# Attention and an ELU feed-forward layer on one core: the order of a batch's first and last pair, halved copies of queries and keys, and a least magnitude that is added inside products

## The chip, the cores and the metric

The kernel runs on one core of a Trainium2 chip. The metric is the device time of one execution in microseconds (us). TensorE (PE, with PEld for its weight loads), VectorE (DVE), ScalarE (ACT), GpSimd (POOL) and SyncE (SP, which issues the transfers) each run their own queue of instructions in order and wait for each other through semaphores.

## The reference

```
scores = q @ k.T / sqrt(64) - log(448)          # q, k, v: 8 batches x 12 heads x 448 x 64, fp32
attn   = 1 / (1 + exp(-scores)) @ v
x      = attn.transpose(0, 2, 1, 3).reshape(3584, 768)
h      = x @ w_in                               # 768 x 2048
g      = where(h > 0, h, exp(min(h, 0)) - 1)
out    = g @ w_out                              # 2048 x 768
```

The sigmoid works on each score by itself, so there is no sum over a row. The two weights come in eight-byte words.

## The kernel before

**Products.** PE multiplies 16-bit numbers. An fp32 operand is split (`split`, L120 to L122) into a high half, written by ACT, and a low half, written by DVE from the source and the high half; a product then takes three matmuls: high by high, low by high, high by low. So that the halves fit, a block is first divided by a power of two near its largest magnitude. `absmax` (L125) finds the maxima per partition (`mx`, and `mt` for queries and keys); `magnitude` (L103) multiplies the unit matrix `eye` by each column of them on DVE (`dg`, L105), and its second part `rest` spreads them over all partitions with one matmul of `ones` by `dg` into `pb` (L110), takes the largest (`al`, L112), puts a floor of 2^-36 under it (L113) and keeps the exponent (`pw`, L114). So a magnitude is DVE, PE, DVE in a row. The weights of the first layer go through `magnitudes` and `sum_magnitude` (L132 to L169), where PE adds up exponents and DVE takes the largest, with the same floor at L165.

**Stages.** A batch has 12 heads in six pairs (hp 0 to 5), a pair four groups of keys (0 to 2 of 128 and a rest of 64). Batch 0 keeps its attention in fp32: PE transposes raw queries and keys into an accumulator `pt` (L337), and one DVE instruction copies both to `early` (L341), from where scores are computed. Beside it the 16 tiles of w_in are loaded and converted; beside batch 0's first layer (`moe1`) w_out is. This prologue is ordered by a scheduler, with its own estimate of times.

From batch 1 on, PE, ACT, DVE and SP run in the order that the code is written in (`manual_schedule`, L690 and after). A batch b is a loop over its six pairs. In each pair: scores of groups 0 and 1 and `soften` for each (sigmoid `sg` on ACT, then the halves `at`, the high one on ACT, L413, the low one on DVE, L414); `third`, which splits queries, keys and values of the next pair (`nat`, `vn`) and turns queries and keys by a transposing transfer; loads of a later pair; some steps of the second layer (`moe2`) of batch b-1; `prepare_pair(n + 2)`, which is `mx`, `mt` and `dg` on DVE; scores and `soften` of groups 2 and 3; more steps; `second`, which is `pb` on PE, `al`, `pw` and the scales; `values` (L433, and L425 for the rest) into `pav`; `finish`, which splits `pav` into `xh`. A step of `moe2` is three matmuls (`po`, L529); `fill` takes a number of them from a stock of 96 in odd batches and 128 in even ones. They are what PE does while ACT and DVE work on a pair. `share` divides what is left by the pairs left. In the last pair `hidden` rescales `xh` (L448 to L451) ahead of the last steps; four steps are kept for after `finish` (`tail`); then `moe1` begins with 16 tiles of 18 matmuls (`ph`, L499), and the batch's own magnitude has its `dg` on DVE ahead of that and its `pb` on PE behind the first tile.

The accumulators: `psc` has two buffers, so scores 3 must wait until ACT has read scores 1.

Of the kernel before, what the change touches and what calls it, by code (L numbers as in the profile page):

```python
# [10 lines left out]
BF16 = mybir.dt.bfloat16  # L11
# [5 lines left out]
ALU = mybir.AluOpType  # L17
# [8 lines left out]
TINY = 2.0**-36  # L26
# [6 lines left out]
def attention_ffn(  # L33
# [9 lines left out]
    nc = tc.nc  # L43
    B, H, S, D = q.shape
    DM, DF = w_in.shape
    P = 128
    NP = H // 2
# [38 lines left out]
    stage, w_in_words = [], []  # L86
    ones = const.tile([P, P], BF16, name="ones")
    nc.vector.memset(ones, 1.0)
    eye = const.tile([P, P], BF16, name="eye")
    nc.vector.tensor_copy(eye, ident)  # L90

# [6 lines left out]
    def magnitude(dst, mx, n):  # L98

        dg = sb.tile([P, n, P], BF16, tag="dg", name="dg", bufs=2)  # L103
        for i in range(n):
            nc.vector.tensor_scalar(dg[:, i], eye, mx[:, i : i + 1], None, op0=ALU.mult)  # L105

        def rest():
            pb = ps.tile([P, 512], F32, tag="pm", name="pb", bufs=3)
            row = pb[:, : n * P].rearrange("p (n x) -> p n x", x=P)
            nc.tensor.matmul(row, ones, dg, start=True, stop=True)  # L110
            al = sb.tile([P, n], F32, tag="al", name="al", bufs=2)
            nc.vector.tensor_reduce(al, row, axis=AX.X, op=ALU.max)  # L112
            nc.vector.tensor_scalar(al, al, TINY, None, op0=ALU.max)  # L113
            nc.vector.tensor_scalar(  # L114
                dst.bitcast(U32), al.bitcast(U32), 0x7F800000, None, op0=ALU.bitwise_and
            )

        return rest
# [13 lines left out]
    def magnitudes(t, lo, hi, hl, sums, start, stop):  # L132


        u, h = t.bitcast(U32), hi.bitcast(F32)


        nc.scalar.activation(t, h, AF.Abs, scale=2.0**-112)


        top = hl.bitcast(U16).rearrange("p a (c t) -> p a c t", t=4)[:, :, :, 1]
        nc.scalar.activation(lo, top, AF.Copy, scale=2.0**-13, bias=2.0**-14 - 0.5)
        nc.vector.scalar_tensor_tensor(
            u, u, 3, lo, op0=ALU.logical_shift_left, op1=ALU.bitwise_or
        )

        top = t.bitcast(BF16).rearrange("p a (c t) -> p a c t", t=2)[:, :, :, 1]
        n = t.shape[1]
        for c in range(n):
            nc.tensor.matmul(  # L150
                sums, ones, top[:, c], start=start and c == 0, stop=stop and c == n - 1
            )
# [8 lines left out]
    def sum_magnitude(dst, sums):  # L161

        m = sb.tile([P, 1], F32, tag="alw", name="alw", bufs=2)
        nc.vector.tensor_reduce(m, sums, axis=AX.X, op=ALU.max)
        nc.vector.tensor_scalar(m, m, TINY, None, op0=ALU.max)  # L165
        nc.vector.tensor_scalar(
            dst.bitcast(U32), m.bitcast(U32), 0x7F800000, None, op0=ALU.bitwise_and
        )
# [125 lines left out]
    def prepare(b, hp, raw, rv, xs):  # L294
# [36 lines left out]
        def transposed(sc):  # L331
            x_scale, s_rest, s_scale = (sc[:, n + i : n + i + 1] for i in range(3))
            if b < EXACT:
                pt = ps.tile([P, 2, 512], F32, tag="psc", name=f"pt{u}", bufs=2)
                pt = pt.rearrange("p a x -> p (a x)")
                for t in range(2 * NC + 1):
                    nc.tensor.transpose(  # L337
                        pt[:, t * P : (t + 1) * P], raw[:, t].rearrange("p h d -> p (h d)"), ident
                    )
                qk = early[:, hp % 2]  # L340
                nc.vector.tensor_copy(qk, pt[:, : 2 * S])  # L341
                return x_scale, 1 / math.sqrt(D), [qk], ([rv], rv[:, 2 * NC :])
            nat = sb.tile([P, 2, 2 * NC + 1, P], F16, tag="nat", name=f"nat{u}")
            for t, n_t, s in (
                (0, NC, sc[:, 1:2]), (NC, 1, s_rest), (NC + 1, NC, sc[:, 2:3])
            ):
                split(
                    nat[:, 0, t : t + n_t], nat[:, 1, t : t + n_t],
                    raw[:, t : t + n_t].rearrange("p t h d -> p t (h d)"), s,
                )  # L350
            qk = sb.tile([P, 2, 2 * NC + 1, P], F16, tag="qk", name=f"qk{u}", bufs=2)
            nc.sync.dma_start_transpose(
                qk.rearrange("p i t x -> p (i t) x"), nat.rearrange("p i t x -> p (i t x)")
            )
            parts = [qk[:, i].rearrange("p t x -> p (t x)") for i in range(2)]

            vn = sb.tile([P, 2, 2 * NC, D], F16, tag="vn", name=f"vn{u}", bufs=2)
            split(vn[:, 0], vn[:, 1], rv[:, : 2 * NC], sc[:, 0:1])
            vr = sb.tile([P, 2, D], F32, tag="vr", name=f"vr{u}", bufs=2)
            nc.gpsimd.tensor_scalar(  # L360
                vr, rv[:, 2 * NC :], sc[:, 0:1], 2.0**ATOP, op0=ALU.mult, op1=ALU.mult
            )
            return x_scale, s_scale, parts, ([vn[:, 0], vn[:, 1]], vr)
# [321 lines left out]
    with tc.manual_schedule(engines={E.PE, E.Activation, E.DVE, E.SP}):  # L685
        for b in range(EXACT, B):
            out_scale(*of_moe2, slice(0, 1 if b == EXACT else NH))
            tiles = moe2(b - 1, g, wo)
            left = NF * NH * (NC + (b - 1) % 2)

            def fill(n):
                nonlocal left
                left -= n
                for _ in range(n):
                    next(tiles, None)

            for hp in range(NP):
                n = b * NP + hp
                share = left // (NP - hp)
                tail = 4 if hp == NP - 1 else 0  # L700
                p = pair_of(n)
                for t in range(2):
                    p.scores(t)
                    p.soften(t)
                third()
                if n + 3 < len(pairs):
                    loaded[n + 3] = load_qk(*pairs[n + 3]), load_v(*pairs[n + 3])

                gap = 8 if hp == 0 else 5
                fill(gap)  # L710
                second = prepare_pair(n + 2)
                for t in range(2, NC + 1):
                    p.scores(t)
                    p.soften(t)
                if b == EXACT and hp < NC:

                    step(3 if hp < NC - 1 else NF)
                if hp == NP - 1:
                    h = hidden(b)
                    next(h)  # L720
                fill(share - gap - tail)
                third = second()
                for t in range(NC + 1):
                    p.values(t)
                p.finish()
                fill(tail)
                if b == EXACT and hp == NC - 1:
                    out_scale(*of_moe2, slice(1, NH))
            of_moe2 = next(h)
# [33 lines left out]
```

## Time and profile before

| | us |
|---|---|
| median of 3 runs | 1271.4 (1270.87 to 1273.9) |
| the profiled execution | 1270.86 |
| its span | 1269.1 |
| PE busy | 1200.2 (95%) |
| DVE busy | 823.4 (65%) |
| ACT busy | 671.8 (53%) |

The span runs from the first to the last instruction of the profile; 1.76 us of the profiled execution lie around it. In a row of the timeline stand the start, the duration, engine, line and operation, the written and read tiles with their shape, how many instructions the row holds, and in brackets the idle time ahead of it and what ended that. Rows of groups have busy time and mean duration in ns, then the idle time ahead. Line numbers in them are those of the kernel before.

### The profile page before, as it was taken

How to read it: one execution, taken by the hardware profiler on the slowest of the kernel's cores; microseconds unless marked ns; L12 is line 12 of the kernel's file. 1: busy time of each engine (PE TensorE's matmuls, PEld its weight loads, DVE VectorE, ACT ScalarE, POOL GpSimd, SP SyncE). 2: the span in 40 equal slices, each digit the busy share in tenths (PEclk: the TensorE clock that was granted, in tenths of full speed). 3: DMA queues.
4: the chain of work that ended last, by engine and by line, in shares of the span. 5: the costliest groups of instructions: out<-in, count | busy, mean ns of one | idle time of the engine just before them, and what ended most of it. 6: DMA issues, size and time to landing. Idle time of an engine off the chain costs nothing.

```text
span 1269.1 us, 19337 instructions
## 1 busy us (share of the span) xinstructions
PE 1200.2 (95%) x7246; PEld 610.5 (48%) x7246; DVE 823.4 (65%) x1872; ACT 671.8 (53%) x1015; POOL 84.1 (7%) x319
## 2 busy tenths in 40 slices
PE   5979868999999999999999999999999999999998
PEld 2324334445555554545455554545455554455565
DVE  5898989765766557775666646885576656765500
ACT  5867777643655337744555436654565435663400
POOL 0011001100000000010000000010000100100000
PEclk9889979999999999999999999999999999999999
DMA  8937423420233103340144201440034401410000
GB/s 229 281 100 222 126 77 80 100 49 1 60 84 89 37 1 83 89 86 1 37 92 92 50 1 43 105 103 7 1 86 92 92 1 22 106 43 7 1 25 26
DMA packets 213407, 89.76 MB, mean 71 GB/s; under 512 B 177472, under 2 KB 209216, under 8 KB 213312
## 3 DMA queue, kind: packets, MB, share of 16 engines
q1 hardware_dynamic: 213312, 88.51, 28.7%
q8 instruction: 57, 0.93, 0.3%
q14 instruction: 38, 0.31, 0.1%
HBM read 58.20 MB, written 11.01 MB: 55 GB/s over the span
## 4 chain that ended last, share of the span: by engine, by line
PE 78%; ACT 8%; DVE 7%; DMA 3%; issue 2%; SPq 2%; DVEq 0%; POOL 0%; ACTq 0%; POOLq 0%
PE ph L499 31%; PE po L529 25%; PE psc L384 7%; PE pav L433 6%; PE po_r L529 5%; PE pav L425 3%; ACT sg L395 2%; DMA stage<-in_moe_w_in_dram 2%; ACT at L413 1%; SPq L262 1%; PE pb L110 1%; ACT L395 1%; ACT e L511 1%; DVE e L514 1%; DMA so<-in_moe_w_out_dram 1%
## 5 line engine op out<-in xcount | busy, mean ns | idle before, releaser
L499 PE MATMUL ph<-xh,wi 128*128 128x448 f16 x2304 | 442.0, 353 | 6.1 <-DVE xh L122 2.4
L529 PE MATMUL po<-wo,g 128*128 128x384 f16 x2304 | 392.9, 328 | 0.0
L529 PEld LDWEIGHTS <-g 128*128 128x128 f16 x2688 | 257.2, 98 | 198.4 <-issue 36.3
L499 PEld LDWEIGHTS <-wi 128*128 128x128 f16 x2304 | 225.3, 98 | 218.4 <-issue 7.6
L511 ACT ACTIVATE e<-ph,msc 128x448 f32<-128x448 f32 x128 | 80.8, 633 | 211.7 <-PE ph L499 211.6
L414 DVE SCALAR_TENSOR_TENSOR at<-sg,at 128x896 f16<-128x896 f32 x126 | 137.2, 1090 | 84.5 <-ACT at L413 84.5
L395 ACT ACTIVATE sg<-psc,bias,sc 128x896 f32<-128x896 f32 (+1 forms) x168 | 166.6, 992 | 1.7
L513 DVE TENSOR_SCALAR e<-e 128x448 f32<-128x448 f32 x128 | 50.3, 394 | 170.8 <-ACT e L511 170.7
L121 ACT ACTIVATE xh<-pav,sc 128x448 f16<-128x448 f32 x48 | 30.3, 632 | 216.7 <-PE pav L425 216.7
L384 PE MATMUL psc<-qk 64*128 64x448 f16 x1008 | 116.6, 355 | 11.4 <-ACT sg L395 11.4
L413 ACT ACTIVATE at<-sg 128x896 f16<-128x896 f32 x126 | 119.8, 951 | 4.1
L121 ACT ACTIVATE g<-e,msc 128x384 f16<-128x384 f32 (+1 forms) x192 | 96.0, 534 | 6.0 <-DVE e L514 4.3
L122 DVE SCALAR_TENSOR_TENSOR g<-e,msc,g 128x384 f16<-128x384 f32 (+1 forms) x192 | 94.6, 521 | 0.6
L514 DVE SCALAR_TENSOR_TENSOR e<-ph,msc,e 128x448 f32<-128x448 f32 x128 | 87.3, 683 | 4.0
L384 PEld LDWEIGHTS <-qk 64*128 64x128 f16 x1008 | 41.7, 97 | 89.7 <-issue 60.2
L433 PE MATMUL pav<-at,vn 128*64 128x448 f16 x756 | 80.2, 357 | 0.0
L324 POOL TENSOR_SCALAR sc<-pw 128x1 f32<-128x1 f32 x42 | 12.4, 295 | 843.5 <-DVE pw L114 790.9
L529 PE MATMUL po_r<-wo,g 128*128 128x384 f16 x384 | 64.7, 326 | 0.0
L122 DVE SCALAR_TENSOR_TENSOR xh<-pav,sc,xh 128x448 f16<-128x448 f32 x48 | 32.7, 680 | 48.7 <-ACT xh L121 48.7
L433 PEld LDWEIGHTS <-vn 128*64 128x64 f16 x756 | 39.4, 110 | 50.0 <-issue 27.8
L122 DVE SCALAR_TENSOR_TENSOR nat<-raw,sc,nat 128x384 f16<-128x384 f32 (+1 forms) x126 | 59.1, 524 | 0.0
L121 ACT ACTIVATE nat<-raw,sc 128x384 f16<-128x384 f32 (+1 forms) x126 | 58.8, 529 | 0.0
(103 smaller groups left out, 852.7 us busy)
## 6 DMA issues: line engine op xcount, KB each, us to landing
stage<-in_moe_w_in_dram SPq DMA_DIRECT2D x16, 768.0 KB, 6.6
raw<-in_q_dram SPq DMA_DIRECT2D x96, 96.0 KB, 3.1
raw<-in_k_dram SPq DMA_DIRECT2D x96, 96.0 KB, 2.6
rv<-in_v_dram SPq DMA_DIRECT2D x48, 192.0 KB, 2.7
out_dram<-o SPq DMA_DIRECT2D x48, 192.0 KB, 2.1
wo<-in_moe_w_out_dram SPq DMA_DIRECT2D x19, 384.0 KB, 4.1
so<-in_moe_w_out_dram SPq DMA_DIRECT2D x13, 384.0 KB, 4.3
raw<-in_q_dram SPq DMA_DIRECT2D x48, 32.0 KB, 2.4
```

Source lines behind the costliest of these rows:

```text
L121: nc.scalar.mul(hi, src, s)
L122: nc.vector.scalar_tensor_tensor(lo, src, s, hi, op0=ALU.mult, op1=ALU.subtract)
L384: nc.tensor.matmul(psc[:, j, :S] if g < NC else psc[rows[j], 0, :S], kk[rows[j], o], qq[rows[j], :S], start=(n == 0), stop=(n == len(parts ...
L395: a = nc.scalar.activation(sg[:, :nb], psc[:, :nb, :S], AF.Sigmoid, bias=bias, scale=self.s_scale)
L413: nc.scalar.mul(hi, sg, 2.0**ATOP)
L414: nc.vector.scalar_tensor_tensor(lo, sg, 2.0**ATOP, hi, op0=ALU.mult, op1=ALU.subtract)
L433: nc.tensor.matmul(pav[rows[j], :S], vv[i][:, j * NC + g], sg[k][:, j], start=(g == 0 and n == 0), stop=False,)
L499: nc.tensor.matmul(ph[:, :S], wi[:, wj, c, f * P : (f + 1) * P], xh[:, c, xj], start=(n == 0), stop=(n == 3 * NK - 1),)
L511: a = nc.scalar.activation(e, ph[:, :S], AF.Exp, scale=inv)
L513: nc.vector.tensor_scalar(e, e, 1.0, -1.0, op0=ALU.min, op1=ALU.add)
L514: nc.vector.scalar_tensor_tensor(e, ph[:, :S], inv, e, op0=ALU.mult, op1=ALU.max)
L529: nc.tensor.matmul(po[:, :HM], lh(gj, f), wo[:, i, f, wj], start=(n == 0), stop=(n == 3 * NF - 1),)
```

## The change

Three things change.

The floor under a magnitude goes into the arithmetic: `dg` becomes `eye` times the maximum plus 2^-36 in the same instruction, and for w_in one more matmul of `ones` by a tile of 2^-36 opens the accumulation. The floor instructions go, except for w_out, whose sums are 384 wide.

The copy of batch 0's queries and keys is made in two halves, queries on ACT and keys on DVE.

The order in the main loop: the first pair takes 11 steps and not 8 at its first fill, and three more in all; there `prepare_pair` comes behind scores and `soften` of groups 2 and 3, and `second` moves into the second pair, between scores 0 and 1 and their `soften`. The last pair has no tail: all its steps come ahead of `pb`. The steps by pair become 19, 15, 15, 15, 16, 16 in odd batches (16 each before) and 24, 20, 21, 21, 21, 21 in even ones (21, 21, 21, 21, 22, 22 before).

```diff
@@ -86,6 +86,8 @@
     stage, w_in_words = [], []
     ones = const.tile([P, P], BF16, name="ones")
     nc.vector.memset(ones, 1.0)
+    tiny = const.tile([P, P], BF16, name="tiny")
+    nc.gpsimd.memset(tiny, TINY)
     eye = const.tile([P, P], BF16, name="eye")
     nc.vector.tensor_copy(eye, ident)
 
@@ -102,7 +104,10 @@
 
         dg = sb.tile([P, n, P], BF16, tag="dg", name="dg", bufs=2)
         for i in range(n):
-            nc.vector.tensor_scalar(dg[:, i], eye, mx[:, i : i + 1], None, op0=ALU.mult)
+
+            nc.vector.tensor_scalar(
+                dg[:, i], eye, mx[:, i : i + 1], TINY, op0=ALU.mult, op1=ALU.add
+            )
 
         def rest():
             pb = ps.tile([P, 512], F32, tag="pm", name="pb", bufs=3)
@@ -110,7 +115,6 @@
             nc.tensor.matmul(row, ones, dg, start=True, stop=True)
             al = sb.tile([P, n], F32, tag="al", name="al", bufs=2)
             nc.vector.tensor_reduce(al, row, axis=AX.X, op=ALU.max)
-            nc.vector.tensor_scalar(al, al, TINY, None, op0=ALU.max)
             nc.vector.tensor_scalar(
                 dst.bitcast(U32), al.bitcast(U32), 0x7F800000, None, op0=ALU.bitwise_and
             )
@@ -146,6 +150,10 @@
 
         top = t.bitcast(BF16).rearrange("p a (c t) -> p a c t", t=2)[:, :, :, 1]
         n = t.shape[1]
+        if n > 1:
+
+            nc.tensor.matmul(sums, ones, tiny, start=True, stop=False)
+            start = False
         for c in range(n):
             nc.tensor.matmul(
                 sums, ones, top[:, c], start=start and c == 0, stop=stop and c == n - 1
@@ -162,7 +170,8 @@
 
         m = sb.tile([P, 1], F32, tag="alw", name="alw", bufs=2)
         nc.vector.tensor_reduce(m, sums, axis=AX.X, op=ALU.max)
-        nc.vector.tensor_scalar(m, m, TINY, None, op0=ALU.max)
+        if sums.shape[1] > P:
+            nc.vector.tensor_scalar(m, m, TINY, None, op0=ALU.max)
         nc.vector.tensor_scalar(
             dst.bitcast(U32), m.bitcast(U32), 0x7F800000, None, op0=ALU.bitwise_and
         )
@@ -338,7 +347,8 @@
                         pt[:, t * P : (t + 1) * P], raw[:, t].rearrange("p h d -> p (h d)"), ident
                     )
                 qk = early[:, hp % 2]
-                nc.vector.tensor_copy(qk, pt[:, : 2 * S])
+                nc.scalar.copy(qk[:, :S], pt[:, :S])
+                nc.vector.tensor_copy(qk[:, S:], pt[:, S : 2 * S])
                 return x_scale, 1 / math.sqrt(D), [qk], ([rv], rv[:, 2 * NC :])
             nat = sb.tile([P, 2, 2 * NC + 1, P], F16, tag="nat", name=f"nat{u}")
             for t, n_t, s in (
@@ -696,34 +706,40 @@
 
             for hp in range(NP):
                 n = b * NP + hp
-                share = left // (NP - hp)
-                tail = 4 if hp == NP - 1 else 0
+                share = left // (NP - hp) + (3 if hp == 0 else 0)
                 p = pair_of(n)
                 for t in range(2):
                     p.scores(t)
+                if hp == 1:
+                    third = second()
+                for t in range(2):
                     p.soften(t)
                 third()
                 if n + 3 < len(pairs):
                     loaded[n + 3] = load_qk(*pairs[n + 3]), load_v(*pairs[n + 3])
 
-                gap = 8 if hp == 0 else 5
+                gap = 11 if hp == 0 else 5
                 fill(gap)
-                second = prepare_pair(n + 2)
+
+                if hp:
+                    second = prepare_pair(n + 2)
                 for t in range(2, NC + 1):
                     p.scores(t)
                     p.soften(t)
+                if not hp:
+                    second = prepare_pair(n + 2)
                 if b == EXACT and hp < NC:
 
                     step(3 if hp < NC - 1 else NF)
                 if hp == NP - 1:
                     h = hidden(b)
                     next(h)
-                fill(share - gap - tail)
-                third = second()
+                fill(share - gap)
+                if hp:
+                    third = second()
                 for t in range(NC + 1):
                     p.values(t)
                 p.finish()
-                fill(tail)
                 if b == EXACT and hp == NC - 1:
                     out_scale(*of_moe2, slice(1, NH))
             of_moe2 = next(h)
```

On DVE, at the start of batch 3 (hp 0; a tile's name ends in its batch and pair, and `at2` is group 2's), before:

```order
L122 SCALAR_TENSOR_TENSOR vn3_1_4696<-rv1_85,sc3_1_4205,vn3_1_4696 128x384
L125 TENSOR_REDUCE mx3_2_4736<-rv0_83 128x1
L125 TENSOR_REDUCE mt3_2_4738<-raw3_2_4090 128x7
L307 TENSOR_REDUCE mx3_2_4736<-mt3_2_4738 128x2
L310 TENSOR_TENSOR mx3_2_4736<-mx3_2_4736,mt3_2_4738 64x1 x2
L105 TENSOR_SCALAR dg_4744<-eye_81,mx3_2_4736 128x128 x3
L414 SCALAR_TENSOR_TENSOR at23_0_4757<-sg23_0_4755,at23_0_4757 128x896
L537 TENSOR_SCALAR o2_0_0_4793<-po2_0_0_4711,osc2_4659 128x384
L112 TENSOR_REDUCE al_4798<-pb_4796 128x3
L113 TENSOR_SCALAR al_4798<-al_4798 128x3
L114 TENSOR_SCALAR pw3_2_4743<-al_4798 128x3
```

and now:

```order
L126 SCALAR_TENSOR_TENSOR vn3_1_4681<-rv1_87,sc3_1_4207,vn3_1_4681 128x384
L424 SCALAR_TENSOR_TENSOR at23_0_4739<-sg23_0_4737,at23_0_4739 128x896
L129 TENSOR_REDUCE mx3_2_4751<-rv0_85 128x1
L129 TENSOR_REDUCE mt3_2_4753<-raw3_2_4080 128x7
L316 TENSOR_REDUCE mx3_2_4751<-mt3_2_4753 128x2
L319 TENSOR_TENSOR mx3_2_4751<-mx3_2_4751,mt3_2_4753 64x1 x2
L108 TENSOR_SCALAR dg_4759<-eye_83,mx3_2_4751 128x128 x3
L547 TENSOR_SCALAR o2_0_0_4778<-po2_0_0_4696,osc2_4644 128x384
L126 SCALAR_TENSOR_TENSOR xh3_3918<-pav3_0_4791,sc3_0_4010,xh3_3918 128x448
L129 TENSOR_REDUCE xs3_3919<-xh3_3918 128x1
L117 TENSOR_REDUCE al_4830<-pb_4828 128x3
```

The low half of group 2 (`at23_0`) moves ahead of the next-but-one pair's maxima and `dg`; `al`, which waits for that pair's `pb`, moves behind `xh` of the first pair.

On PE, where that `pb` (`pb_4796` before, `pb_4828` now) stands, before:

```order
L529 MATMUL po2_0_0_4711<-wo_966,g_917 128x384
L110 LDWEIGHTS ones_79
L110 MATMUL pb_4796<-dg_4744,ones_79 128x384
L433 LDWEIGHTS vn3_0_4085
L433 MATMUL pav3_0_4811<-at03_0_4672,vn3_0_4085 64x448
```

and now:

```order
L394 MATMUL psc13_1_4821<-qk3_1_4679 128x448
L115 LDWEIGHTS ones_79
L115 MATMUL pb_4828<-dg_4759,ones_79 128x384
L539 LDWEIGHTS g_917
L539 MATMUL po2_1_0_4781<-wo_965,g_917 128x384
```

It stood between the first pair's last step and its values; it stands now behind the second pair's scores 0 and 1, ahead of that pair's first step.

On DVE at the end of batch 3 (hp 5; `rr` and `xs` belong to the rescaling), before:

```order
L450 TENSOR_SCALAR xh3_3924<-xh3_3924,rr3_5617 128x896 x5
L451 TENSOR_TENSOR xs3_3925<-xs3_3925,rr3_5617 128x5
L112 TENSOR_REDUCE al_5648<-pb_5646 128x3
L113 TENSOR_SCALAR al_5648<-al_5648 128x3
L114 TENSOR_SCALAR pw4_1_5591<-al_5648 128x3
L318 RECIPROCAL sc4_1_5652<-pw4_1_5591 128x3
L282 TENSOR_TENSOR xs4_5412<-xs4_5412,pw4_1_5591 128x1
L285 RECIPROCAL xs4_5412<-xs4_5412 128x1
L122 SCALAR_TENSOR_TENSOR xh3_3924<-pav3_5_5661,sc3_5_5315,xh3_3924 128x448
L125 TENSOR_REDUCE xs3_3925<-xh3_3924 128x1
L537 TENSOR_SCALAR o2_2_1_5696<-po2_2_1_5568,osc2_4659 128x384
```

and now:

```order
L460 TENSOR_SCALAR xh3_3918<-xh3_3918,rr3_5597 128x896 x5
L461 TENSOR_TENSOR xs3_3919<-xs3_3919,rr3_5597 128x5
L547 TENSOR_SCALAR o2_2_1_5638<-po2_2_1_5548,osc2_4644 128x384
L117 TENSOR_REDUCE al_5643<-pb_5641 128x3
L118 TENSOR_SCALAR pw4_1_5571<-al_5643 128x3
L327 RECIPROCAL sc4_1_5646<-pw4_1_5571 128x3
L291 TENSOR_TENSOR xs4_5393<-xs4_5393,pw4_1_5571 128x1
L294 RECIPROCAL xs4_5393<-xs4_5393 128x1
L126 SCALAR_TENSOR_TENSOR xh3_3918<-pav3_5_5655,sc3_5_5296,xh3_3918 128x448
L129 TENSOR_REDUCE xs3_3919<-xh3_3918 128x1
L466 TENSOR_REDUCE rr3_5597<-xs3_3919 128x1
```

The eviction of the last steps (`o2_2_1`), which stood behind `xh`, now stands ahead of `al`, and the floor (L113) is gone.

On ACT in the prologue, rows now, with what each waits for (`pt_1` is the second pair's accumulator, `stage` and `wi` belong to w_in):

```order
L142 ACTIVATE stage<-stage 128x768 [waits DMAHW3_49]
L146 ACTIVATE stage<-stage 128x768
L125 ACTIVATE wi<-stage,swi_155 128x6x128 [waits Pool_49]
L142 ACTIVATE stage<-stage 128x768 [waits DMAHW4_49]
L146 ACTIVATE stage<-stage 128x768
L350 COPY early<-pt_1_192 128x448 [waits PE_49]
L405 ACTIVATE sg_0_209<-psc_0_206,bias 128x896 [waits PE_49]
```

and on DVE, around the other half of the same copy:

```order
L291 TENSOR_TENSOR xs_114<-xs_114,pw_1_180 128x1 [waits DVE_49]
L147 SCALAR_TENSOR_TENSOR stage<-stage 128x768 [waits DMAHW4_49,Activation_49]
L294 RECIPROCAL xs_114<-xs_114 128x1 [waits DVE_49]
L351 COPY early<-pt_1_192 128x448 [waits Activation_49]
L172 TENSOR_REDUCE alw<-si_226 128x1 [waits PE_49]
L165 SCALAR_TENSOR_TENSOR stage<-stage 128x768
```

The copy of the queries is in ACT's queue behind the work on a further tile of w_in, and the copy of the keys on DVE waits for ACT.

## The prediction

> **What bounds the kernel now.** I read the page's totals first, then busy time by stretch of the span.
>
> ```profile
> span 1269.1 us, 19337 instructions
> PE 1200.2 (95%) x7246; PEld 610.5 (48%) x7246; DVE 823.4 (65%) x1872; ACT 671.8 (53%) x1015; POOL 84.1 (7%) x319
> 0.00:98.00 98.00, 72.86 (x358) 29.74 (x359) 77.66 (x203) 63.75 (x81) 8.10 (x33) 0.93 0.71 198
> 98.00:200.00 102.00, 80.98 (x424) 38.87 (x423) 90.12 (x196) 80.73 (x147) 11.42 (x29) 0.91 0.46 137
> 200.00:1202.00 1002.00, 983.64 (x6083) 504.39 (x6081) 648.09 (x1461) 525.10 (x783) 64.56 (x259) 1.00 0.25 55
> ```
>
> A stretch's columns are its length, then busy time of PE, PEld, DVE, ACT and POOL, the granted clock, DMA share and GB/s. Two regimes are to be seen. Up to 200 us no engine is full, and VectorE (DVE) is the busiest: 77.66 of 98 in the prologue (batch 0's attention and w_in's conversion) and 90.12 of 102 in batch 0's first FFN stage. From 200 on, in the main loop, TensorE (PE) works 983.64 of 1002 us: only its idle 18.4 us can be won there. So I listed PE's waits in that stretch in order of time. These rows stand for them, with the first and the last of each kind; column two is the duration, the bracket the idle time ahead and what ended it.
>
> ```profile
> 260.77 0.32 PE L110 MATMUL pb<-dg,ones 128*128 128x384 bf16 x1 [1.90 <-DVE dg L105]
> 850.92 0.32 PE L110 MATMUL pb<-dg,ones 128*128 128x384 bf16 x1 [1.90 <-DVE dg L105]
> 327.49 0.76 PE L384 MATMUL psc<-qk 64*64 64x448 f16 x6 [1.22 <-ACT sg L395]
> 917.64 0.76 PE L384 MATMUL psc<-qk 64*64 64x448 f16 x6 [1.22 <-ACT sg L395]
> 480.01 0.76 PE L384 MATMUL psc<-qk 64*64 64x448 f16 x6 [1.03 <-ACT sg L395]
> 1070.17 0.76 PE L384 MATMUL psc<-qk 64*64 64x448 f16 x6 [1.03 <-ACT sg L395]
> 486.75 0.32 PE L110 MATMUL pb<-dg,ones 128*128 128x384 bf16 x1 [1.97 <-DVE dg L105]
> 781.02 0.32 PE L110 MATMUL pb<-dg,ones 128*128 128x384 bf16 x1 [1.97 <-DVE dg L105]
> 1076.90 0.32 PE L110 MATMUL pb<-dg,ones 128*128 128x384 bf16 x1 [1.97 <-DVE dg L105]
> ```
>
> They lie only in the pairs that the change reorders. The last pair (hp 5) of batches 1, 3 and 5 waits 1.9 for dg; the first pair (hp 0) of 2, 4 and 6 waits 1.22 for scores 3; the first pair of 3, 5 and 7 waits 1.03 for scores 3 and 1.97 for dg. That is 3×1.9 + 3×1.22 + 3×(1.03+1.97) = 18.4.
>
> **The first pair.** Its three added steps of moe2 must fill these waits. What a step lasts, and what DVE and ACT do at batch 3's first pair:
>
> ```profile
> 480.70 4.07 PE L529 MATMUL po<-wo,g 128*128 128x384 f16 x24
> 483.77 0.95 ACT L413 ACTIVATE at<-sg 128x896 f16<-128x896 f32 x1
> 483.84 0.68 DVE L125 TENSOR_REDUCE mx<-rv 128x1 f32<-128x512 f32 x1
> 486.11 0.58 DVE L105 TENSOR_SCALAR dg<-eye,mx 128x128 bf16<-128x128 bf16 x3
> 486.61 1.08 DVE L414 SCALAR_TENSOR_TENSOR at<-sg,at 128x896 f16<-128x896 f32 x1
> 488.13 0.55 DVE L112 TENSOR_REDUCE al<-pb 128x3 f32<-128x384 f32 x1
> 487.00 1.89 PE L433 MATMUL pav<-at,vn 128*64 128x448 f16 x18
> 489.77 1.31 PE L384 MATMUL psc<-qk 64*128 64x448 f16 x12
> ```
>
> 24 matmuls are 8 steps, 4.07/8 = 0.51 each. Three more ahead of scores 2 and 3 are 1.53 us, above both 1.03 and 1.22: those waits go, and the last step of the pair ends 0.5 later, at 485.27 for 484.77 (480.70+4.07). No pb follows now but the values. They need at2's low half only for their last third, at 485.27 + 2/3×1.89 = 486.5. ACT has the high half at 484.72 (483.77+0.95), and the low half, now ahead of mx, takes 1.08: done at 485.8, 0.7 early. The 1.97 goes.
>
> What is late next is dg: from mx's start to dg's end DVE takes 486.69−483.84 = 2.85, so 485.8+2.85 = 488.65. PE asks for it after values (1.89), the remainder's matmuls and two scores (1.31): 485.27+1.89+0.95+1.31 = 489.4. It is hidden by 0.7; were it later, the excess would count in each of six batches. On DVE, al (0.55) and five small operations behind it wait for that pb and now stand ahead of the second pair's own splits. That can make those start up to half a us late, 3 us in six batches; I take nothing, since ACT's splits of the same pair, one after another, reach DVE's queue later still.
>
> **The last pair.** All 11 steps stand ahead of pb, not 7: 4×0.51 = 2.04 covers 1.9. The price is the lost tail between values and the first FFN stage, seen at batch 2's end:
>
> ```profile
> 416.41 2.11 PE L529 MATMUL po_r<-wo,g 128*128 128x384 f16 x12
> 417.49 0.67 DVE L122 SCALAR_TENSOR_TENSOR xh<-pav,sc,xh 128x448 f16<-128x448 f32 x1
> 419.31 0.26 DVE L105 TENSOR_SCALAR dg<-eye,rr 128x128 bf16<-128x128 bf16 x1
> 418.36 3.57 PE L499 MATMUL ph<-xh,wi 128*128 128x448 f16 x18
> 421.77 0.22 PE L110 MATMUL pb<-dg,ones 128*128 128x128 bf16 x1
> ```
>
> The four steps (2.11) stood behind the values, which end at 416.41; now the FFN's first tile does. It uses the last pair's xh only in the last of its six parts, 5/6×3.57 = 3.0 after its start. xh's low half came at 418.16, 1.75 after the values: free. Magnitude's dg came at 419.57, 3.2 after them, and pb is asked for 3.4 after the tile's start (421.77−418.36): free too, by 0.2. If it slips, 0.3 in each of seven batches is 2 us.
>
> **Shares.** 96 steps are now 19, 15, 15, 15, 16, 16 in odd batches, where each pair had 16; even ones have 24, 20, 21, 21, 21, 21. Does a pair of 15 hide the chain scores, ACT, DVE, dg? At batch 3's third pair:
>
> ```profile
> 513.43 0.58 DVE L105 TENSOR_SCALAR dg<-eye,mx 128x128 bf16<-128x128 bf16 x3
> 514.07 0.32 PE L110 MATMUL pb<-dg,ones 128*128 128x384 bf16 x1
> ```
>
> dg ends at 514.01 and pb starts at 514.07: with 16 steps PE comes just as dg does. With 15 it must wait for the step it lacks: about 0.5 for hp 2 and for hp 3. The second pair has an extra pb (0.32) from the first, so it loses 0.17. That is −1.13 in batches 3, 5, 7 and −1.0 in batch 1. Pairs of 20 and more have 2 us in hand.
>
> Sum of the loop: batch 1, 1.9−1.0 = 0.9; 2, 4 and 6, 3×1.22 = 3.7; 3 and 5, 1.03+1.97+1.9−1.13 = 3.8 each; 7, 3.0−1.13 = 1.9. Together −14.1.
>
> **One half-clock window.** Behind the 1.97 wait at 781, and not behind the other two, the same matmuls were slow:
>
> ```profile
> 781.35 2.54 PE pav L433 x18
> 783.88 1.79 PE pav L425 x2
> 488.82 1.02 PE L425 MATMUL pav<-sg,vr 128*128 128x448 f32 x2
> ```
>
> 2.54 against 1.89 and 1.79 against about 0.9 net: 1.5 lost. Without the wait I expect none: −1.5, between 0 and that. The Trainium skill, "TensorE: Matmul & The Clock Gate", section "Why this matters for your kernels", asks for an idle gap of about 3 us before the clock drops. By it the window would have another cause and stay, and the sum would be 1.5 higher; this trace shows a drop in one of three waits of 1.97, so I side with the row.
>
> **The start of batch 1** has two waits of its own, while w_out's last halves are converted:
>
> ```profile
> 196.46 0.74 PE L384 MATMUL psc<-qk 64*128 64x448 f16 x6 [2.51 <-ACT sg L395]
> 198.43 1.17 PE L384 MATMUL psc<-qk 64*64 64x448 f16 x6 [1.23 <-ACT sg L395]
> ```
>
> The three more steps could cover 1.5 of the 3.74; against it, the conversions' halves stand behind the reordered dg. I take −0.5, from −3.7 to +2.
>
> **Prologue.** The diff turns six copies on DVE into halves on two engines and drops the small floor ops.
>
> ```profile
> L341 DVE COPY early<-pt 128x896 f32<-128x896 f32 x6 | 6.5, 1090 | 8.2 <-PE pt L337 8.0
> L113 DVE TENSOR_SCALAR al<-al 128x3 f32<-128x3 f32 (+1 forms) x56 | 9.2, 164 | 1.6
> L121 ACT ACTIVATE xh<-pav,sc 128x448 f16<-128x448 f32 x48 | 30.3, 632 | 216.7 <-PE pav L425 216.7
> L122 DVE SCALAR_TENSOR_TENSOR xh<-pav,sc,xh 128x448 f16<-128x448 f32 x48 | 32.7, 680 | 48.7 <-ACT xh L121 48.7
> 21.42 0.90 ACT L142 ACTIVATE stage<-stage 128x768 uint32<-128x768 uint16 x1
> 17.77 1.09 DVE L341 COPY early<-pt 128x896 f32<-128x896 f32 x1 [0.96 <-PE pt L337]
> ```
>
> A half on either engine costs about 0.6 (632 and 680 ns for such a PSUM read). DVE saves 6×(1.09−0.6) = 2.9 and, with 22 floors (16 tiles, 6 pairs) at 0.16, 3.5: at most −6.4, if every bit counts. But the changed order has each DVE half wait for the ACT half, so the pair takes 1.2 in a row where 1.09 stood, and ACT's second copy stands behind the third w_in tile, whose part ends at 22.32 where the copy began at 17.77: +4.55 if it were on the path. DVE is full through most of the prologue, so freed time should count somewhat: −1, between −6.4 and +4.6. The Trainium skill, "ScalarE: Activation LUTs", section "Rules for kernel authors", would leave plain arithmetic on VectorE, up to about three times faster per element there in bf16. By that an ACT half would be an estimated 1.6 us, and the six copies 6.6 longer in total; the two rows above, 632 on ACT and 680 on DVE, do not agree for fp32 from PSUM. From 98 to 200 and in dg's added operand I take nothing.
>
> Sum: −14.1−1.5−0.5−1.0 = −17.1. The profiled execution took 1270.86 (span 1269.1 and 1.76 around), so 1253.8; the median of the runs is 0.5 above it, so 1254.
>
> **Rivals.**
> Prologue delays. Each copy that comes k times late on ACT's queue costs 4.55 on the path of batch 0. Two give back 9 us: 1264, chance 0.14 for one or two (from 1259). Three or four end at 1268 to 1273, no change: 0.05. The chip is slower only from five on: six give 27.3−1 above 1254, about 1281, since scores of batch 0, and w_in's conversion behind them, start that late: 0.04. For it: ACT runs its instructions in order. Against: in the trace ACT worked 63.75 of 98 us, so most copies find it free.
> More gain. If a 15-step pair loses nothing (PE's latency there being shorter than I read) 4.4 comes back, and with −6.4 for the prologue it is 1244: 0.11 for 1249 or less.
> dg slower. The added operand could put dg in a slower form: +0.1 on each of three in some 18 pairs without slack, 5.4, so 1259. Nothing in the trace shows it; 0.05 within the main case.
> The change does not do what it says in one place: the two halves do not run side by side. This is priced above.
>
> **How the numbers follow.** Main case 1250 to 1259 with 0.66, at 1254. Range 1245 to 1265: it holds the main case, one or two late copies and most of the further gain; about 0.17 is outside. A measurement here tells 0.3%, 3.8 us, from no change: faster is below 1267.6 (0.66+0.14+0.11 = 0.91), same up to 1275.2 (0.05), slower 0.04.
>
> **What would show it.** Right: no waits above 0.5 us ahead of pb or scores 3 in first and last pairs; new waits of 0.5 ahead of pb in hp 2 and hp 3 of odd batches; no half-clock window at batch 5's start; the first main-loop pair within 5 us of its old place. Wrong: a prologue ending over 5 us later, waits for dg at hp 1 or in the FFN's first tile, or dg over 0.3 us each.

## The result: the loop gained what was forecast, and the prologue gave a third of it back

The kernel with the change takes 1260.77 us (1259.97 to 1260.92), the one before 1272.62 beside it: a ratio of 0.9906, with a 95% interval of 0.9889 to 0.9924. So it is faster, by 11.85 us; 1254 was forecast. The profiled execution took 1260.89 with a span of 1259.1; against the span of before, 1269.1, that is 10.0 less, where 17.1 was forecast. (The profiled execution of before, 1270.86, lies 1.76 under the median beside it, so the traces show some 1.9 less gain than the medians.)

The page's totals after the change, and its busy time by stretch (length; PE, PEld, DVE, ACT, POOL; clock, DMA share, GB/s):

```profile
span 1259.1 us, 19310 instructions
PE 1199.5 (95%) x7262; PEld 609.6 (48%) x7262; DVE 813.9 (65%) x1800; ACT 675.1 (54%) x1021; POOL 97.0 (8%) x320
0.00:98.00 98.00, 68.14 (x343) 27.46 (x344) 70.33 (x165) 66.89 (x87) 9.13 (x32) 0.95 0.73 197
98.00:200.00 102.00, 85.81 (x451) 41.62 (x449) 87.72 (x196) 74.89 (x139) 10.11 (x24) 0.93 0.44 135
```

In the first 98 us DVE is busy 70.33 for 77.66 before: the work was taken off it (and some now falls behind 98), but no time came of that. To see where time went, take one instruction that every batch has once, and call its start the batch's mark: the `pb` of the batch's own magnitude, behind the FFN's first tile. Batch 0's mark is called the prologue's end below. Of PE's timeline before the change, batches 0 to 5:

```profile
102.14 0.22 PE L110 MATMUL pb<-dg,ones 128*128 128x128 bf16 x1
269.05 0.22 PE L110 MATMUL pb<-dg,ones 128*128 128x128 bf16 x1
421.77 0.22 PE L110 MATMUL pb<-dg,ones 128*128 128x128 bf16 x1
563.33 0.22 PE L110 MATMUL pb<-dg,ones 128*128 128x128 bf16 x1
716.05 0.22 PE L110 MATMUL pb<-dg,ones 128*128 128x128 bf16 x1
859.21 0.22 PE L110 MATMUL pb<-dg,ones 128*128 128x128 bf16 x1
```

And with the change:

```profile
107.78 0.22 PE L115 MATMUL pb<-dg,ones 128*128 128x128 bf16 x1
273.26 0.22 PE L115 MATMUL pb<-dg,ones 128*128 128x128 bf16 x1
424.68 0.22 PE L115 MATMUL pb<-dg,ones 128*128 128x128 bf16 x1
562.69 0.22 PE L115 MATMUL pb<-dg,ones 128*128 128x128 bf16 x1
714.12 0.22 PE L115 MATMUL pb<-dg,ones 128*128 128x128 bf16 x1
852.13 0.22 PE L115 MATMUL pb<-dg,ones 128*128 128x128 bf16 x1
```

The differences tell the story. The prologue ends 5.64 later (107.78 for 102.14). From there to batch 1's mark takes 165.48 for 166.91, 1.4 less. Batch 2 takes 151.42 for 152.72 (−1.30), batch 3 138.01 for 141.56 (−3.55), batch 4 151.43 for 152.72 (−1.29), batch 5 138.01 for 143.16 (−5.15). Batches 6 and 7 give 1.28 and 1.63 in the same way. Together −10.0.

In the loop, PE's waits of before are gone, and new ones stand where the prediction put them: ahead of `pb` in hp 1, 2 and 3 of batch 3.

```profile
501.70 0.32 PE L115 MATMUL pb<-dg,ones 128*128 128x384 bf16 x1 [0.58 <-DVE dg L108]
515.35 0.32 PE L115 MATMUL pb<-dg,ones 128*128 128x384 bf16 x1 [0.43 <-DVE dg L108]
529.00 0.32 PE L115 MATMUL pb<-dg,ones 128*128 128x384 bf16 x1 [0.43 <-DVE dg L108]
```

### The profile page after: what moved, and what is told of

Its sections match the earlier page's. It is cut to its first block, busy times and chain, and to the rows that moved or that the text cites. A ratio compares the mean times of both kernels' runs of the same rounds, so it can differ in the third digit from the quotient of the medians.

```text
span 1259.1 us, 19310 instructions
## 1 busy us (share of the span) xinstructions
PE 1199.5 (95%) x7262; PEld 609.6 (48%) x7262; DVE 813.9 (65%) x1800; ACT 675.1 (54%) x1021; POOL 97.0 (8%) x320
## 4 chain that ended last, share of the span: by engine, by line
PE 73%; DVE 10%; ACT 7%; DMA 5%; issue 3%; SPq 2%; POOL 1%; DVEq 0%; ACTq 0%; POOLq 0%
PE ph L509 31%; PE po L539 20%; PE psc L394 6%; PE pav L443 6%; PE po_r L539 5%; PE pav L435 3%; ACT sg L405 3%; DMA stage<-in_moe_w_in_dram 1%; ACT at L423 1%; DVE mt L129 1%; DVE mx L129 1%; DVE nat L126 1%; DMA wo<-in_moe_w_out_dram 1%; PE pb L115 1%; DVE dg L108 1%
```

## The experiments

**Parts alone.** Theory: the reordered loop gained as forecast, and the two edits that reach into the prologue lost 6 us there, above all the halves. Rival: the floor edits lose it. A third, that the reordered loop itself delays w_out's conversion, was put to the first run. For each run, the part of the diff that it keeps (the order of pairs; the halves; the floors):

```diff
+                share = left // (NP - hp) + (3 if hp == 0 else 0)
...
+                gap = 11 if hp == 0 else 5
```

> Only the order of the first and last pair is changed; floors and the single copy stay as before. Theory (the main loop gained what was forecast, and 6 us were lost ahead of it by the two edits in the prologue): 16 to 17 us faster than before, about 1255, with the prologue row for row as before (batch 0's own pb near 102.1). Rival (the reordered loop itself starts 6 us late, since batch 1's first pair delays w_out's conversion): about 10 us faster, as the whole change.

Measured: 1258.41, ratio 0.9881 (0.9868 to 0.9895): 14.9 less than the 1273.33 of before in that series, a little short of the 16 to 17 expected. The prologue ended at 102.73, and up to 98 us every engine's queue has the order of before. So the loop didn't lose the 6 us, and the order of pairs alone is at least as good as the whole change.

```diff
-                nc.vector.tensor_copy(qk, pt[:, : 2 * S])
+                nc.scalar.copy(qk[:, :S], pt[:, :S])
+                nc.vector.tensor_copy(qk[:, S:], pt[:, S : 2 * S])
```

> Only the copy of batch 0's queries and keys is halved between ACT and DVE. Theory (the halves make the scheduler lay the prologue's queues anew, with a w_out load ahead of the third pair's loads, and the copies wait for ACT): 5 to 7 us slower than before, batch 0's own pb near 107 to 109. Rival (the floor edits do it): within 1 us of before.

Measured: 1277.93, ratio 1.0045 (1.0031 to 1.0058), 4.6 slower; prologue's end at 110.12. The rival falls. The theory has the direction; both its numbers are just missed, 4.6 for 5 to 7 and 110.12 for 107 to 109.

```diff
+                dg[:, i], eye, mx[:, i : i + 1], TINY, op0=ALU.mult, op1=ALU.add
...
-            nc.vector.tensor_scalar(al, al, TINY, None, op0=ALU.max)
...
+            nc.tensor.matmul(sums, ones, tiny, start=True, stop=False)
```

> Only the floor is moved into dg and into the sums of w_in. Theory: between 0 and 3.5 us faster than before (22 operations of 0.16 us leave DVE in the prologue). Rival (the floor edits move the prologue's queues for the worse): 5 to 7 us slower.

Measured: 1275.89, ratio 1.002 (1.001 to 1.003), 2.6 slower; prologue's end at 106.75. The theory missed, and the rival's 5 to 7 was too much: this edit too delays the prologue, though on DVE it only takes operations off (PE gets 16 short matmuls more). By the sum of the three parts the whole would be 14.9−4.6−2.6 = 7.7 faster; it is 11.85. About half of the 4.2 between them lies in the loop: with the new order of pairs, batches 3, 5 and 7 take 138.01, 138.01 and 137.43 from mark to mark without the floor and 138.77, 138.78 and 137.97 with it, 2.1 less together, while with the old order batch 3 takes 141.54 without it and 141.56 with it. The rest may come of something that each part sets anew: the scheduler's order.

```diff
+                nc.scalar.copy(qk[:, :512], pt[:, :512])
+                nc.vector.tensor_copy(qk[:, 512:], pt[:, 512 : 2 * S])
```

> The whole change, but the copy is cut at column 512, where the accumulator's first bank ends, so that ACT and DVE read different banks. If the loss in the prologue is that the two halves run one after the other (about 0.6 us in each of six pairs, and what hangs on it): 3 us or more faster than the whole change, about 1257. If it is where ACT's half and the loads stand in their queues: within 2 us of it, 1259 to 1262.

Measured: 1254.23 (1253.85 to 1254.98), ratio 0.9852 (0.9839 to 0.9865), 6.5 faster than the whole change and the fastest of all. It looked like the price of two reads one after the other. But this cut, too, had given the scheduler a new order, so the run didn't tell the two apart. Nor do the reads overlap in it: in all six pairs DVE's half starts after ACT's has ended.

**The order written out.** For that, the next kernels keep their instructions and take the queue order from another kernel. Ahead of the main loop each instruction of the five engines gets a dependency of order alone on the one that stands ahead of it in that other kernel (1,276 to 1,370 of them; those that the other kernel doesn't have are placed by the scheduler):

```diff
+        for a, b in zip(queue, queue[1:]):
+            tc.add_manual_dep(seen[b], a, mybir.DependencyInfo(
+                mybir.DependencyClass.NoSync, mybir.DependencyReason.DATA), ...)
```

The theory is now that the order of the queues sets the prologue; its rivals, that an edit costs by itself.

> Floors moved into dg and into w_in's sums as in the floor-only run (2.6 us slower), but all that is ordered by the scheduler stands in every engine's queue in the order of the kernel before. Theory (the scheduler's new order costs, not the edit): 0 to 3.5 us faster than before. Rival (the added operand or the extra matmul costs by itself): 2 to 3 us slower, as unpinned.

Measured: 1275.04, ratio 1.0014 (1.0001 to 1.0026).

> Queries copied by ACT and keys by DVE as in the halves-only run (4.6 us slower), with every other instruction in the order of before; DVE's half stands where the whole copy stood, and the scheduler places ACT's half alone. Theory (new order): within 1.5 us of before. Rival (two reads one after the other, and ACT's queue, cost by themselves): 4 to 6 us slower, as unpinned.

Measured: 1274.16, ratio 1.0015 (1.0003 to 1.0027).

> As the pinned halves, but cut at column 512 so that the two engines read different banks of the accumulator. If the reads one after the other cost: 2 to 4 us faster than the pinned halves. If only the order of the queues counts: within 1 us of them.

Measured: 1275.31, ratio 1.0018 (1.0005 to 1.003).

These three were less clear than hoped. In the order of before, the halves cost 1.2 by the medians and not 4.6, for the theory. The pinned floors are 2.1 slower by the medians, against the 0 to 3.5 faster that the theory expected. The cut at 512 is 1.2 slower than the pinned halves, but says nothing on parallel reads, for it has none: DVE's half still waits for ACT's and starts as that ends (19.91+0.56 = 20.47).

```profile
19.91 0.56 ACT L394 COPY early<-pt 128x512 f32<-128x512 f32 x1
20.50 0.56 DVE L395 COPY early<-pt 128x384 f32<-128x384 f32 x1 [3.59 <-ACT early L394]
```

Why it waits wasn't tried. So no run here has the two reads side by side, and what that would gain stays open. Kernels with the old loop also spread widely (before from 1270.65 to 1277.19 in this series), those with the new one by 1 to 4 us. The spread goes with the clock: of the 55 executions of before beside these experiments, the 6 with a mean granted clock of 0.981 took 1276.5 in the median, the 18 at 0.983 took 1273.86 and the 12 at 0.985 took 1272.07. Differences of 1 to 2 us between kernels with the old loop are therefore not settled by these medians; so I went on with the new loop.

> The whole change with the cut at column 512, and the instructions ahead of the main loop in the order of before. Theory: the loop's gain of about 15 us and, with nothing lost ahead of it, 1255 to 1258. Rival (the scheduler's own order with that cut, 19 us faster than before, was luck that the order of before doesn't have): as well 1255 to 1258; under 1254 would say that floors and parallel halves gain by themselves.

Measured: 1259.59 (1258.72 to 1260.42), ratio 0.9897 (0.9882 to 0.9911). Above the 1255 to 1258 that was expected, and 5.4 above the same instructions in the scheduler's order for them. That pair is the cleanest answer so far: the instructions are the same, and only their order ahead of the loop differs.

> The whole change with its own cut at 448, and all that stands ahead of the main loop in the queue order that the scheduler had made for the cut at 512 (1254.2). Theory (the order of the queues sets the prologue): 1254 to 1256. Rival (two reads of one bank, one after the other, cost by themselves): 1258 to 1261.

Measured: 1255.38 (1254.42 to 1255.42), ratio 0.9859 (0.9844 to 0.9874). The whole change, unaltered, is 5.4 faster when its prologue stands in another order, and the ranges of the two don't meet. The rival's 1258 to 1261 doesn't come: with its reads one after the other, the change still reaches 1255.38. What such reads cost isn't priced by the 1254.23 of the cut at 512, for there they are one after the other too.

> The whole change with its own cut at 448, and the prologue in the queue order of before. Theory: 1258.5 to 1260, as the cut at 512 in that order (1259.6) and the order alone (1258.4). Rival (one read after the other costs by itself): 1261 or more.

Measured: 1259.42 (1257.21 to 1260.31), ratio 0.9889 (0.9875 to 0.9904). As the theory had it, and the rival's 1261 or more falls.

> Only the reordered pairs, with the old floors and the single copy on DVE, in that same queue order of the prologue. Theory (order alone): 1254 to 1256, against 1258.4 in the order of before. Rival (the work taken from DVE is what gained): 1258 to 1260.

Measured: 1261.56 (1259.77 to 1263.04), ratio 0.9909 (0.9894 to 0.9924). The theory in its plain form falls here, and the time is above the rival's 1258 to 1260 too: the good order doesn't help the old instructions, it costs them 3 us against the 1258.41 in their own. By the traces they lose it in the prologue, which ends at 106.49 for 102.73. Against the change in that order they lose another 2.2 in batches 3, 5 and 7, where they still have the floor. An order is good for the instructions that it was made for. Why these lose in it wasn't tried.

By instructions and order, all with the new loop:

| | order of before | order made for the cut at 512 | the scheduler's own |
|---|---|---|---|
| old floors, one copy | 1258.41 | 1261.56 | as the first column |
| the change, cut at 448 | 1259.42 | 1255.38 | 1260.77 |
| the change, cut at 512 | 1259.59 | 1254.23 | as the second column |

The table has the loop in it, where the floor alone is worth 2.1. By the traces, ahead of batch 1's mark, the change at 448 comes to 272.25 in the first order and 267.78 in the second, the old instructions to 268.83 and 271.00. So it is neither the order nor the instructions but the pair of them: either order is 3 us worse for the other's instructions. Of the 4.5 between the two orders of the change, 1.4 lies ahead of batch 0's mark (104.81 for 103.38) and 3.0 behind it, in the stretch where w_out is converted.

**Where the order bites.** The whole change in its own order loses most of its 5.4 ahead of batch 0's mark, and here one can look for the place. Up to 73.5 us it and the same change in the other order are level (scores at 73.63 and 73.43). Then, in its own order, by engine (SP's rows have the issue and what held it; `raw` and `rv` are loads of queries, keys and values, `stage` of w_in):

```profile
61.96 8.15 SPq L190 DMA_DIRECT2D stage<-in_moe_w_in_dram  x2
70.21 0.50 SPq L256 DMA_DIRECT2D rv<-in_v_dram  x1
79.42 0.62 SPq L275 DMA_DIRECT2D raw<-in_k_dram  x1
76.14 0.98 ACT L405 ACTIVATE sg<-psc,bias 128x896 f32<-128x896 f32 x1
86.54 0.63 ACT L405 ACTIVATE sg<-psc,bias 128x448 f32<-128x448 f32 x1 [4.46 <-PE psc L394]
80.30 0.69 DVE L129 TENSOR_REDUCE mx<-rv 128x1 f32<-128x512 f32 x1 [3.01 <-DMA raw<-in_k_dram]
81.83 0.25 DVE L108 TENSOR_SCALAR dg<-eye,mx 128x128 bf16<-128x128 bf16 x1
82.13 0.26 PE L115 MATMUL pb<-dg,ones 128*128 128x128 bf16 x1 [1.39 <-DVE mx L319]
```

The same instructions in the order made for the cut at 512 (line numbers are about 50 higher, for the table of the order):

```profile
60.23 0.53 SPq L239 DMA_DIRECT2D stage<-in_moe_w_in_dram  x1
67.33 0.37 SPq L305 DMA_DIRECT2D rv<-in_v_dram  x1
69.59 0.37 SPq L239 DMA_DIRECT2D stage<-in_moe_w_in_dram  x1
75.23 0.62 SPq L324 DMA_DIRECT2D raw<-in_k_dram  x1
73.72 0.99 ACT L454 ACTIVATE sg<-psc,bias 128x896 f32<-128x896 f32 x1
75.68 0.69 DVE L179 TENSOR_REDUCE mx<-rv 128x1 f32<-128x512 f32 x1
77.61 0.25 DVE L158 TENSOR_SCALAR dg<-eye,mx 128x128 bf16<-128x128 bf16 x1
79.57 0.23 PE L165 MATMUL pb<-dg,ones 128*128 128x128 bf16 x1
103.38 0.22 PE L165 MATMUL pb<-dg,ones 128*128 128x128 bf16 x1
```

In the slower order (the whole change's own) two loads of w_in stand ahead of the values' load on SP and hold its queue for 8.15 us (probably until a staging buffer is free, which the rows don't show); the values' load is issued at 70.21 for 67.33 and the last keys at 79.42 for 75.23. On DVE, which works in order, the maxima wait 3.01 for a load (80.30 for 75.68; the profile names the keys' load, though `mx` reads `rv`), so `dg` is late, PE's `pb` waits 1.39, and the scores that stand behind `pb` on PE come so late that ACT idles 4.46. On ACT the sigmoid comes 2.4 later, behind conversions of w_in. The prologue ends at 107.78 for 103.38. None of it is the price of an instruction.

Two things weaken this reading. PE's granted clock was half from 75.34 to 85.58 in the slower order and from 74.12 to 77.53 in the other, so the same four matmuls of `pav` take 1.76 at 83.81 there and 0.97 at 80.90 here; how much of the 4.4 is the clock, and how much of the clock comes of the waits, isn't separated. And a prologue's end is that of one execution: the next run has the good order and the instructions of the cut at 512, and its profiled execution, the longest of five at 1259.47, ends its prologue at 106.99 where the kernel that the order comes from ended at 103.21. What shows the order's price is the times of the runs; the rows show where it can arise.

**One step moved.** The fastest kernel with one step less in the first pair and one more in hp 1 of odd batches:

```diff
-                share = left // (NP - hp) + (3 if hp == 0 else 0)
+                share = left // (NP - hp) + (2 if hp == 0 else 1 if hp == 1 and b % 2 else 0)
...
-                gap = 11 if hp == 0 else 5
+                gap = 10 if hp == 0 else 5
```

> The kernel with the cut at 512 in its own queue order, with one step less in a batch's first pair (10 at its first fill) and one more in the second pair of odd batches, so that odd batches have 18, 16, 15, 15, 16, 16. By the waits in the whole change's trace (0.58 ahead of pb in the second pair, 0.43 in each of the next two): the 0.58 goes in each of three or four odd batches, 1.5 to 2.3 us faster than 1254.2. Rival (the first pair has no step to give, scores 3 or dg wait again): no gain, or up to 2 us slower.

Measured: 1256.81 (1255.75 to 1259.47), 2.6 slower than 1254.23: the rival, by a little more than its 2 us. In its trace scores 3 wait again in even batches, and hp 1's wait didn't shrink:

```profile
328.54 0.76 PE L443 MATMUL psc<-qk 64*64 64x448 f16 x6 [0.24 <-ACT sg L454]
499.11 0.32 PE L165 MATMUL pb<-dg,ones 128*128 128x384 bf16 x1 [0.63 <-DVE dg L158]
```

Each batch is 0.2 to 0.3 longer, 1.7 in six; the rest lies ahead of the loop, where nothing was changed. hp 1 has one step more and its wait is no shorter, so it isn't short of PE's steps: by these rows its chain on DVE sets the end.

## Why the prediction was right in the loop and wrong ahead of it

**First and last pair.** Right. The waits of 1.22, 1.03, 1.97 and 1.9 are gone. Batch 2's −1.30 answers to 1.22, batch 3's −3.55 to the forecast 3.8.

**Shares.** Right for hp 2 and hp 3: 0.43 where 0.5 was forecast, in three batches and in batch 1. The mis-sized term is hp 1, 0.17 forecast and 0.58 measured, 0.41 more in each of three batches. The step that failed is "I take nothing, since ACT's splits of the same pair, one after another, reach DVE's queue later still". DVE's and ACT's timelines at batch 3's second pair:

```profile
492.56 0.61 DVE L129 TENSOR_REDUCE xs<-xh 128x1 f32<-128x448 f16 x1
493.08 0.55 DVE L117 TENSOR_REDUCE al<-pb 128x3 f32<-128x384 f32 x1
...
496.79 0.91 ACT L125 ACTIVATE nat<-raw,sc 128x128 f16<-128x128 f32 x2 [0.70 <-POOL sc L331]
```

`al` is read at 493.08, behind `xh` and its maximum, where its `pb` was there at 492.34 (492.00+0.34); the scales from it come through POOL, and ACT waits 0.70 for them. The floor stood in this chain: with it, in the kernel that has only the new order, hp 1 waits 1.12:

```profile
497.80 0.32 PE L110 MATMUL pb<-dg,ones 128*128 128x384 bf16 x1 [1.12 <-DVE dg L105]
```

So in the loop the floor edit is worth 0.54 by this wait in each of batches 3, 5 and 7 (0.54 to 0.77 from mark to mark), which the prediction priced at nothing.

**The half-clock window.** Right for these two executions, with some luck in it. Batch 5 gained 5.15, 1.6 more than batch 3, for the 1.5 forecast. Now in that place, behind no wait, the values take their usual time:

```profile
777.42 1.89 PE L443 MATMUL pav<-at,vn 128*64 128x448 f16 x18
779.24 1.02 PE L435 MATMUL pav<-sg,vr 128*128 128x448 f32 x2
```

In the kernel with only the floors changed, the window falls behind the third wait of 1.97, in batch 7:

```profile
1080.70 0.32 PE L114 MATMUL pb<-dg,ones 128*128 128x384 bf16 x1 [1.97 <-DVE dg L107]
1080.95 3.04 PE L440 MATMUL pav<-at,vn 128*64 128x448 f16 x18
1083.93 1.51 PE L432 MATMUL pav<-sg,vr 128*128 128x448 f32 x2
```

In the main loop beyond batch 1, each of the six traces with these waits has one such window, and none of the eight without them has any; the trace of the pinned floors has one more in batch 1, behind the wait of 1.90 there. The Trainium skill, "TensorE: Matmul & The Clock Gate", section "Why this matters for your kernels", which would have left the time as it was, doesn't hold for 1.97 here.

The luck is in which wait it is. The granted clock in these traces changes only on a grid of 3.41 us. In the trace of before, the stretch from 778.90 to 782.31 has the whole wait of 1.97 in it (PE busy 1.44 of 3.41), and from 782.31 to 785.72 the clock is half. Carry the grid back: a border at 485.35 cuts the first wait of 1.97, the stretch behind the border still has PE busy 2.02, and the clock stays full. So it is in all six traces from 208 us on: each window follows a stretch with 1.90 idle or more, all six stretches with 1.96 or more are followed by one, and of three with 1.90 one is. The grid falls elsewhere in each execution, so the 1.5 is the price of a window in batch 5 in this trace of before, and another execution can have it elsewhere, or more than one.

**The start of batch 1.** −0.5 was forecast there and −0.9 for the rest of the batch; from the first step of `moe2` to batch 1's mark it measured −2.5 (104.01 for 106.52). But the step behind the −0.5, that three more steps cover part of the two waits, is wrong: they stand in the second pair as before.

```profile
202.73 0.74 PE L394 MATMUL psc<-qk 64*128 64x448 f16 x6 [2.56 <-ACT sg L405]
204.70 1.03 PE L394 MATMUL psc<-qk 64*64 64x448 f16 x6 [1.22 <-ACT sg L405]
```

The waits that the added steps did cover are in the first pair, ahead of w_out's sums, where 1.42 is gone; before and now:

```profile
168.69 0.80 PE L150 MATMUL so<-wo,ones 128*128 128x384 bf16 x2 [1.42 <-DVE wo L143]
175.38 0.80 PE L158 MATMUL so<-wo,ones 128*128 128x384 bf16 x2
```

PE's waits in that pair shrink from 10.34 to 8.26 in all, 2.1 where 0.5 was forecast, which more than makes up the extra 1.1. The 1.42 is covered by steps; that the others shrink by 0.66 has no cause shown here. 1.1 was lost in the FFN stage just ahead of it, and what of w_out's conversion is done there needn't be done here.

**The tail, dg's second operand.** Right: the tail's loss shows nowhere, and dg takes 250 ns for 251:

```profile
L108 DVE TENSOR_SCALAR dg<-eye,mx 128x128 bf16<-128x128 bf16 x132 | 26.1, 250 | 1.4
```

**The prologue.** Wrong. The step that failed is "DVE is full through most of the prologue, so freed time should count somewhat: −1, between −6.4 and +4.6": it measured +5.64 by the two traces, outside both ends, and the first FFN stage behind it another 1.1 (from batch 0's mark to the first step of `moe2` 61.47 for 60.39). Against the trace with the new loop alone, whose prologue has the order of before and ends at 102.73, it is +5.05. A busy share of 77.66 in 98 was read as a bound, but the stretch hangs on waits along in-order queues, and the freed DVE time brought nothing in any order but one (batch 1's mark at 267.78 there, for 268.83 with the old instructions in their own order).

The time, 1260.77, lies above the main case and within the rival of one or two late copies (1259 to 1264), and the copies did come late: ACT's second at 22.18, where 22.32 was named for 17.77 before. But that lateness doesn't set the time. The sixth pair's copy on DVE, 61.74 before, in the whole change, in the same change in the order made for 512, and in the order of before:

```profile
72.97 0.61 DVE L351 COPY early<-pt 128x448 f32<-128x448 f32 x1
72.76 0.61 DVE L400 COPY early<-pt 128x448 f32<-128x448 f32 x1
64.50 0.62 DVE L399 COPY early<-pt 128x448 f32<-128x448 f32 x1 [0.38 <-ACT early L398]
```

The first two are as late, and their prologues end at 107.78 and 103.38; the third is 8 us earlier and ends at 104.81. So the range held, and the time fell into a rival's part of it by another mechanism: that is luck. (The rival's sum for six late copies, 27.3−1 above 1254, is 1280 and not 1281; with the −1 taken back, as it is for two, 1282.) The copies themselves are cheap.

```profile
L351 DVE COPY early<-pt 128x448 f32<-128x448 f32 x6 | 3.7, 613 | 0.0
L350 ACT COPY early<-pt 128x448 f32<-128x448 f32 x6 | 3.1, 521 | 5.5 <-PE pt L346 5.5
```

521 ns on ACT and 613 on DVE are what was forecast (0.6). The Trainium skill's "ScalarE: Activation LUTs", section "Rules for kernel authors", has DVE up to about three times faster in bf16, which no copy here tests; for fp32 out of the accumulator the 6.6 us estimated from it didn't come. What I left out as a term is that any edit to a stretch that a scheduler orders moves every queue in it; the moved queues were in front of me, and a price for them needed the loads' places on SP, which I didn't read.

**The signs.** Two of those named for being wrong came: a prologue ending over 5 us later (5.64) and a wait for dg at hp 1 (0.58). Of those for being right, one didn't hold: the first main-loop pair starts at 169.25 for 162.53, 6.7 from its old place. Another didn't hold in batch 1, whose first pair waits 1.06 for scores 3 (0.96 before).

## What to carry to other kernels

Where the order is written out by hand, waits read from the trace add up: from batch 2 on, forecast and measurement agreed to 0.3 us a batch. Where a scheduler orders the work, an edit's price has the new order's in it, here 5.4 us between two orders of the same instructions; compare the queues, loads above all, and write the order out to separate the two. An order that suits one set of instructions can cost another 3 us. A busy share of 80% wasn't a bound here: each engine works in order and waits for the others.

## What the runs showed of the hardware

A wait of 1.97 us on PE was at times followed by 3.41 us at half the granted clock (782.31 to 785.72 before; 18 matmuls in 2.54 or 3.04 for 1.89). In the main loop that happened behind one of three such waits, not always the same one: the one that lay whole within one 3.41 us stretch of the clock's grid. Once a wait of 1.90 was followed so too.

A copy of 128x448 fp32 out of the accumulator took 521 ns on ACT and 613 on DVE. A second operand in dg (multiply, then add) cost nothing: 250 ns for 251.
